# Longformer attention and a SwiGLU block on one core: gathers for two batches, an opening with early scores, and eight attention bursts per batch

## The chip, the core and the metric

The kernel runs on one NeuronCore of a Trainium2 chip. A core has TensorE (PE in the profile: matmuls; PEld is its weight load), VectorE (DVE), ScalarE (ACT), GpSimd (POOL) and SyncE (SP), and 16 DMA engines that move data between HBM and the on-chip memory SBUF. Matmuls write to PSUM, eight banks of 2 KB a partition, which DVE and ACT read. Each engine takes its instructions in program order and waits on semaphores of others. POOL and SP issue the DMAs here. The metric is device time in microseconds (us).

## What is computed

Eight batches of eight heads with 576 tokens and head size 64 go through attention with a sliding window of 32 tokens on either side and eight global tokens, which see and are seen by all. Its output, 4608 rows of 512, goes through a gated FFN of width 1536.

```python
B, H, S, D = q.shape                       # 8, 8, 576, 64
scores = np.matmul(q, k.transpose(0, 1, 3, 2)) / np.sqrt(D)
mask = np.abs(pos[:, None] - pos[None, :]) <= 32
mask = mask | is_global[:, None] | is_global[None, :]
attn = softmax(np.where(mask, scores, -1e9))
x = np.matmul(attn, v).transpose(0, 2, 1, 3).reshape(B * S, H * D)
g = x @ w_gate                             # 512 -> 1536
out = (g * sigmoid(g) * (x @ w_val)) @ w_out
```

## The kernel before

**Units and gaps.** The FFN takes the rows in nine chunks of 512. A chunk is 16 units: twelve gates (`gate`, L702: four matmuls `pg` and four `pv` of 512 columns; then tanh on ACT and two products `gv` and `h` on DVE) and four output strips (`outp`, L769: twelve matmuls `po`, a copy `osb` on ACT and a store on SP). The units are numbered from 0, sixteen a chunk (the first two do nothing, since their work is in the opening). Behind unit n the program puts what `gaps[n]` holds: the steps of the attention of a later batch, which run on TensorE as a burst between two units. The order on every engine is the order of the program (`manual_schedule`, L61).

**One batch of attention** (`attention(b)`, L340) has these steps. `step_T` (batches 1 and 2; batch 0 has `step_T0`) transposes k and q on TensorE, one pair of heads at a time; later batches get them by DMA transposes of a bf16 copy in DRAM. `step_GT` transposes the gathered global rows `kqm`. `step_S2` and `step_SG` are the scores of global queries and global keys, each with an exp on ACT and a mask product on DVE (`p2`, `pg`). `step_P2T` transposes p2, on TensorE or, from batch 4, by a DMA on SP. `step_AV2` multiplies by v and DVE makes `gv` of it. `step_S(0..3)` are the windowed scores of half the heads and half the rows, `step_S(4)` the last 64 rows; each has an exp and a product with `band` on DVE. `step_AV(tp)` makes 128 rows of output from two of these, `gv` and `pg`, and `normalise` on DVE divides into `xa`; `step_AV8` makes the last 64 rows. `step_X` and `step_X8` transpose xa into `xT`, which the FFN reads: on TensorE with an ACT copy in batches 0 and 1, by a DMA on SP later. `vb` (L636) is v shifted by 64 rows, made by two DMAs on SP.

**PSUM.** The pool `pf` has four single banks for the FFN (tag "f"). The pools `psc` (tag "sc") and `pm` (tag "m") hold one tile of two banks each. A step that takes a tile there waits until the last reader of the tile before is through. `mtile` gives batch 0 a tile of pf, later batches one of pm.

**Global rows.** `gather(b)` (L236) issues two indirect DMAs on POOL, one for k and one for q, with the row numbers `gofs[:, b]`. A partition stands for a head and a global token; `gather_mask` (L247) multiplies by `mka` so that each pair of heads keeps its own half, on POOL, for batch 0 on DVE. `gofs` is computed by a row of small DVE instructions (L180 to L215).

**The opening.** Ahead of unit 0, batch 0 runs as a list written by hand (L654 to L665), in which `M(...)` places the mask products and normalisations (`p*`, `xa*`) apart from their steps. `warm(n)` are matmuls on ones whose result nobody reads. Then `first_gates` (L720) begins the FFN with the rows that are ready. POOL issues the loads in this order: k and q of the first four heads, k of the other four, the two gathers, q of the other four, v, two thirds of w_gate and w_val, and then `loads_b` (L284): k and q of batch 1, the last third of the weights, the gather of batch 1, v, and w_out.

Of the kernel before, what the change touches and what calls it, by code (L numbers as in the profile page):

```python
# [9 lines left out]
FP32 = mybir.dt.float32  # L10
BF16 = mybir.dt.bfloat16
I32 = mybir.dt.int32
# [14 lines left out]
def kernel(  # L27
# [112 lines left out]
    def load_0(name, hg):  # L140
# [12 lines left out]
                   allow_small_or_imprecise_dtypes=True)  # L153
    bofs_f = const.tile([P, B], FP32)
    nc.gpsimd.iota(bofs_f, pattern=[[H * S, B]], base=0, channel_multiplier=0,
                   allow_small_or_imprecise_dtypes=True)
# [7 lines left out]
    ones = const.tile([P, CH], BF16)  # L164
    nc.vector.memset(ones, 1.0)
    act0 = const.tile([P, 1], FP32)
# [3 lines left out]
    nc.vector.memset(mt[:, WIN + S : KC], 0.0)  # L170
    def clear(i):
        nc.vector.memset(kT_bufs[i][:, :, 0:WIN], 0.0)
        nc.vector.memset(kT_bufs[i][:, :, WIN + S : KC], 0.0)
        nc.vector.memset(va_bufs[i][:, :, :, D : D + 2], 0.0)
        nc.vector.memset(va_bufs[i][:, :, :, D : D + 1], 1.0)
        nc.vector.memset(va_bufs[i][0:WIN, 0, :, :], 0.0)
        nc.vector.memset(va_bufs[i][P - WIN : P, 4, :, :], 0.0)

# [10 lines left out]
    dmask = const.tile([P, HP, 2], FP32)  # L189
    gofs = const.tile([P, B], I32)  # L190

    nc.vector.tensor_tensor(out=dmask, in0=oh16[:, :, 0, :], in1=oh16[:, :, 1, :], op=ALU.add)
    dmh = const.tile([P, 2, 2], FP32)
    nc.vector.tensor_tensor(out=dmh, in0=dmask[:, 0:2], in1=dmask[:, 2:4], op=ALU.add)
    clear(0)
    tmp8h = const.tile([P, NG], FP32)
# [18 lines left out]
    nc.vector.tensor_scalar(out=gofs, in0=bofs_f, scalar1=hrow, scalar2=None, op0=ALU.add)  # L215
    mka = const.tile([P, 2, 2], FP32)
    nc.vector.tensor_reduce(
        out=mka, in_=oh16.rearrange("p h a r -> p a r h"), axis=AX.X, op=ALU.add
    )
    asel = const.tile([P, 2], FP32)  # L220
    nc.vector.tensor_reduce(out=asel, in_=mka, axis=AX.X, op=ALU.add)
    R2 = (WIN + 0.5) ** 2
# [12 lines left out]

    def gather(b):  # L236
        kg = gw.tile([P, D], FP32, tag="kg", name="kg")
        qg = gw.tile([P, D], FP32, tag="qg", name="qg")
        for dst, src in ((kg, k), (qg, q)):
            nc.gpsimd.indirect_dma_start(  # L240
                out=dst, out_offset=None,
                in_=src.rearrange("b h s d -> (b h s) d"),
                in_offset=bass.IndirectOffsetOnAxis(ap=gofs[:, b : b + 1], axis=0),
            )
        return kg, qg, gw.tile([P, 2, 2, D], BF16, tag="kqm", name="kqm")

    def gather_mask(kg, qg, kqm, eng=None):  # L247
        for a, src in ((0, kg), (1, qg)):
            (eng or nc.gpsimd).tensor_tensor(
                out=kqm[:, a], in0=bc(src, [[0, 2], [1, D]]),  # L250
                in1=bc(mka[:, a, :], [[1, 2], [0, D]]), op=ALU.mult,
            )
        return kqm

# [12 lines left out]

    kqms = [None] * B
    g0 = gather(0)
    load_0("q", 1)  # L270
    load_v(0)
# [11 lines left out]
    load_wgv(1)  # L283
    def loads_b():  # L284
        loaded[1] = new_qk()
        load_qk_part(1, loaded[1], 0)
        load_qk_part(1, loaded[1], 1)
        load_wgv(2)
        g1 = gather(1)
        load_v(1, range(0, 3))  # L290
        kqms[1] = gather_mask(*g1)
        load_v(1, range(3, 5))
        for i in range(4):
            nc.gpsimd.dma_start(
                out=wo_sb[:, 3 * i : 3 * i + 3, :],
                in_=moe_w_out[3 * P * i : 3 * P * (i + 1), :].rearrange(
                    "(fc p) m -> p fc m", p=P
                ),
            )
# [40 lines left out]
    def attention(b):  # L340
# [50 lines left out]
        def step_GT():  # L391
# [200 lines left out]
        def step_X(tp):  # L592
# [19 lines left out]
            nc.scalar.copy(out=xT[:, :, c0 : c0 + P], in_=ps)  # L612

        def step_X8():
            if b >= XB:
# [23 lines left out]
        def vb0(t):  # L639
            st["vb"] = load_vb(0)  # L640
            nc.vector.tensor_copy(out=st["vb"][0:64, 0:2], in_=va[64:128, 0:2])
            nc.vector.tensor_copy(out=st["vb"][64:128, 0:2], in_=va[0:64, 1:3])
            nc.sync.dma_start(out=st["vb"][0:64, 2:4], in_=va[64:128, 2:4])
            nc.sync.dma_start(out=st["vb"][64:128, 2:4], in_=va[0:64, 3:5])

        L = lambda f, *a: (lambda: f(*a))
        if b == 0:
# [3 lines left out]
            def kqm0():  # L651
                kqms[0] = gather_mask(*g0, eng=nc.vector)
# [43 lines left out]

# [112 lines left out]
    def gather_now(b):  # L809
        held[b] = gather(b)  # L810

    def mask_now(b):
        kqms[b] = gather_mask(*held[b])

# [66 lines left out]
```

## Time and profile before

| | |
|---|---|
| median of 4 runs | 366.82 us (366.18 to 368.96) |
| the profiled execution | 365.92 us |
| its span, first to last instruction | 364.2 us |
| granted TensorE clock in the records | 1.000 |
| busy: PE, DVE, ACT, POOL | 350.7, 233.4, 153.4, 97.5 us |

The profile's page cuts the span into 40 slices and gives each engine's busy share in tenths. Of the page, these are the rows of TensorE, DVE and POOL:

```profile
PE   3799999999999999999999999999999999999996
DVE  6666686368934884588548854885488638724850
POOL 7934545924544001540245024100000000000000
```

A slice is 9.1 us. TensorE is busy in all but the first two and the last. The costliest groups of instructions (line, engine, operation, tiles, shapes, count; then busy us and mean ns of one; then the engine's idle time before it) begin so:

```profile
L713 PE MATMUL pg<-xT,wg_sb 128*128 128x512 bf16 x420 | 108.3, 380 | 0.0
L713 PE MATMUL pv<-xT,wv_sb 128*128 128x512 bf16 x420 | 107.8, 379 | 0.0
L746 DVE SCALAR_TENSOR_TENSOR gv<-th,pg 128x512 bf16<-128x512 bf16 x107 | 73.3, 685 | 40.5 <-ACT th L744 39.7
L744 ACT ACTIVATE th<-pg 128x512 bf16<-128x512 f32 x107 | 63.9, 598 | 79.5 <-PE pg L713 69.8
L774 PE MATMUL po<-wo_sb,h 128*128 128x512 bf16 x420 | 94.5, 379 | 0.0
```

Matmuls overlap, so the 380 ns of one is not the time between two of them. How many instructions a group has and the starts in the timeline tell that time.

### The profile page before, as it was taken

The page shows a single profiled execution, that of the slowest core. Times are in us where ns is not written, and L with a number is a line of the kernel's source. Part 1 is how long each engine was busy: PE and PEld are TensorE (multiplying, and loading weights), DVE is VectorE, ACT ScalarE, POOL GpSimd, SP SyncE. Part 2 cuts the span into 40 slices and gives each one's busy share as a digit, 9 for nine tenths or more (in the row PEclk, how much of TensorE's full clock was granted, in tenths as well). Part 3 has the DMA queues.
Part 4 walks back from the last instruction along what each step waited for, and adds up shares of the span by engine and source line. Part 5 has one row for each costly group of instructions (what it writes and reads, how often), then busy time and mean ns, then how long its engine had stood idle before and what let it go on. Part 6 is the DMA issues. An engine that isn't in the chain of part 4 may idle for free.

```text
span 364.2 us, 7867 instructions
## 1 busy us (share of the span) xinstructions
PE 350.7 (96%) x3226; PEld 171.2 (47%) x3226; DVE 233.4 (64%) x469; ACT 153.4 (42%) x238; POOL 97.5 (27%) x114
## 2 busy tenths in 40 slices
PE   3799999999999999999999999999999999999996
PEld 2556444554444454444444444444444444444444
DVE  6666686368934884588548854885488638724850
ACT  5635673457323551345225532452254333323322
POOL 7934545924544001540245024100000000000000
DMA  7999999999999927999999998932350131011002
GB/s 105 141 209 204 132 194 199 185 204 146 138 171 173 187 55 115 138 148 153 153 136 139 142 149 145 165 71 58 116 88 0 45 117 23 0 59 58 0 13 104
DMA packets 141636, 43.51 MB, mean 119 GB/s; under 512 B 126368, under 2 KB 135840, under 8 KB 141600
## 3 DMA queue, kind: packets, MB, share of 16 engines
q0 software_dynamic: 93824, 19.40, 63.2%
q1 hardware_dynamic: 47776, 23.60, 31.6%
q8 instruction: 25, 0.41, 0.5%
q14 instruction: 11, 0.09, 0.1%
HBM read 38.28 MB, written 15.34 MB: 147 GB/s over the span
## 4 chain that ended last, share of the span: by engine, by line
PE 84%; DMA 10%; POOL 3%; DVE 1%; issue 1%; ACT 0%; DVEq 0%; POOLq 0%
PE po L774 25%; PE pg L713 24%; PE pv L713 23%; DMA kg<-in_k_dram,gofs 4%; DMA wg_sb<-in_moe_w_gate_dram 3%; PE ps_av L557 3%; PE ps_s L495 3%; DMA vb<-va 2%; POOL va L102 1%; PE ps_av L548 1%; DMA va<-in_v_dram 1%; PE po L761 1%; PE ps_t L377 1%; PE ps_av L464 1%; PE ps_s L429 1%
## 5 line engine op out<-in xcount | busy, mean ns | idle before, releaser
L713 PE MATMUL pg<-xT,wg_sb 128*128 128x512 bf16 x420 | 108.3, 380 | 0.0
L713 PE MATMUL pv<-xT,wv_sb 128*128 128x512 bf16 x420 | 107.8, 379 | 0.0
L746 DVE SCALAR_TENSOR_TENSOR gv<-th,pg 128x512 bf16<-128x512 bf16 x107 | 73.3, 685 | 40.5 <-ACT th L744 39.7
L744 ACT ACTIVATE th<-pg 128x512 bf16<-128x512 f32 x107 | 63.9, 598 | 79.5 <-PE pg L713 69.8
L774 PE MATMUL po<-wo_sb,h 128*128 128x512 bf16 x420 | 94.5, 379 | 0.0
L750 DVE TENSOR_TENSOR h<-gv,pv 128x512 bf16<-128x512 bf16 x107 | 73.6, 688 | 11.5 <-PE pg L713 0.5
L713 PEld LDWEIGHTS <-wv_sb 128*128 128x128 bf16 x424 | 41.5, 98 | 50.0
L774 PEld LDWEIGHTS <-h 128*128 128x128 bf16 x420 | 39.9, 98 | 46.4
L102 POOL DMA_DIRECT2D va<-in_v_dram x40 | 35.3, 990 | 95.5 <-PE ps_av L557 86.6
L713 PEld LDWEIGHTS <-wg_sb 128*128 128x128 bf16 x424 | 37.0, 98 | 40.9 <-issue 1.7
L779 ACT ACTIVATE osb<-po 128x512 f32<-128x512 f32 x35 | 20.9, 597 | 81.2 <-PE po L774 79.2
L503 ACT ACTIVATE pe<-ps_s 128x1024 bf16<-128x1024 f32 (+1 forms) x40 | 37.5, 939 | 18.2 <-PE ps_s L495 17.4
L509 DVE TENSOR_TENSOR pt<-pe,band 128x1024 bf16<-128x1024 bf16 (+1 forms) x40 | 25.5, 637 | 21.1 <-ACT pe L503 20.6
L524 DVE TENSOR_REDUCE den<-ps_av 128x8 f32<-128x16 f32 (+1 forms) x40 | 6.7, 169 | 35.7 <-PE ps_av L557 33.0
L530 DVE TENSOR_TENSOR xa<-ps_av,den 128x512 bf16<-128x512 f32 (+1 forms) x40 | 25.5, 638 | 1.6 <-DMA xT<-xa 0.2
L495 PEld LDWEIGHTS <-kT 64*128 64x128 bf16 x576 | 11.3, 98 | 15.9 <-issue 14.8
L495 PE MATMUL ps_s<-qT,kT 64*128 64x64 bf16 x576 | 16.2, 196 | 1.1 <-ACT pe L503 1.1
L557 PE MATMUL ps_av<-va,pt 128*64 128x66 bf16 x256 | 15.0, 202 | 0.0
L557 PE MATMUL ps_av<-vb,pt 128*64 128x66 bf16 x256 | 14.8, 202 | 0.1
L109 POOL DMA_DIRECT2D qf<-in_q_dram x5 | 14.0, 2802 | 0.0
L557 PEld LDWEIGHTS <-pt 128*64 128x64 bf16 x512 | 11.4, 114 | 4.6 <-issue 0.7
L109 POOL DMA_DIRECT2D kf<-in_k_dram x5 | 11.4, 2285 | 6.4 <-DMA qf<-in_q_dram 6.2
(123 smaller groups left out, 214.4 us busy)
## 6 DMA issues: line engine op xcount, KB each, us to landing
out_dram<-osb SPq DMA_DIRECT2D x35, 256.0 KB, 2.1
vb<-va SPq DMA_DIRECT2D x14, 264.0 KB, 4.6
va<-in_v_dram POOLq DMA_DIRECT2D x24, 128.0 KB
kf<-in_k_dram POOLq DMA_DIRECT2D x5, 576.0 KB, 10.0
qf<-in_q_dram POOLq DMA_DIRECT2D x5, 576.0 KB, 19.5
k_bf<-in_k_dram POOLq DMA_DIRECT2D x6, 288.0 KB
q_bf<-in_q_dram POOLq DMA_DIRECT2D x6, 288.0 KB, 4.3
va<-in_v_dram POOLq DMA_DIRECT2D x16, 96.0 KB, 10.6
```

Source lines behind the costliest of these rows:

```text
L102: nc.gpsimd.dma_start(out=va[lo:hi, u, :, 0:D], in_=vs[t0 + lo : t0 + hi])
L109: nc.gpsimd.dma_start(out=t, in_=src[b].rearrange("h s d -> s h d"))
L495: nc.tensor.matmul(out=ps[:, par, 64 * slot : 64 * slot + 64], lhsT=kT[r : r + 64, hp, 64 * t : 64 * t + P], rhs=qTs[b][r : r + 64, hp, 64 ...
L503: nc.scalar.activation(out=pe, in_=ps[:, :, 0 : 64 * ns].rearrange("p r (s c) -> p r s c", c=64), func=AF.Exp, scale=SCALE,)
L509: mult = lambda: nc.vector.tensor_tensor(out=pt.rearrange("p r s c -> p (r s) c"), in0=pe.rearrange("p r s c -> p (r s) c"), in1=bc(band, ...
L530: nc.vector.tensor_tensor(out=xa.rearrange("p (g h) d -> p g h d", g=g), in0=bc(ps, pst + [[1, D]]), in1=bc(den, [[4, g], [1, 4], [0, D]]) ...
L557: nc.tensor.matmul(out=ps[64 * e : 64 * e + 64, hg, hl, :], lhsT=pt[:, hl % 2, 4 * (hl // 2) + 2 * (tp % 2) + e, :], rhs=(va if e == 0 els ...
L713: nc.tensor.matmul(out=ps[:, 0:n], lhsT=w[:, cc, P * fc : P * (fc + 1)], rhs=xT[:, cc, t0 : t0 + n], start=(cc == 0), stop=(cc == NCC - 1),)
L744: nc.scalar.activation(out=th[:, 0:n], in_=pg[:, 0:n], func=AF.Tanh, scale=0.5)
L746: nc.vector.scalar_tensor_tensor(out=gv[:, 0:n], in0=th[:, 0:n], scalar=1.0, in1=pg[:, 0:n], op0=ALU.add, op1=ALU.mult,)
L750: nc.vector.tensor_tensor(out=st["h"][:, fc, 0:n], in0=gv[:, 0:n], in1=pv[:, 0:n], op=ALU.mult)
L774: nc.tensor.matmul(out=po, lhsT=st["h"][:, fc, P * ts : P * (ts + 1)], rhs=wo_sb[:, fc, :], start=(fc == 0), stop=(fc == NFC - 1),)
```

## The change

The gathers: `gather(i)` serves batches 2i and 2i+1. `bofs_f` and `gofs` get a row for k and one for q; the partitions that hold the unused half of a head pair are given the row numbers of the next batch (`hb`), so the k gather brings k rows of one batch in one half and of the next in the other, and `gather_mask(b, ...)` picks by `(a + b) % 2`. `step_GT` swaps the halves of odd batches in two copies. `mka` and `asel` are computed ahead of `gofs`. `kqm` has four buffers. The opening's first gather follows the second q load, and batch 1 has no gather of its own; its mask runs on POOL at the start of `loads_b`.

The opening: two blocks of scores, S(0) and S(2), run right behind the first four heads' transposes, the other heads' k copies go to DVE, both their q copies to ACT. `clear` is split: batch 1's memsets go to POOL (in `loads_b`), batch 0's k borders and `ones` move into `tables_a`. The second half of `vb` is made by two ACT copies, not by two DMAs on SP. Five warm matmuls stand where there were four.

The bursts: in batches 1 and 2, and from 3 on, the steps are grouped into fewer gaps. Batch 1 begins one gap later (3, not 2) and transposes xa two strips at a time (`step_X01`). From batch 3 the gap numbers are written out. Tiles: S2 of batch 0 and S4 of batch 2 take psc; AV of batches 1 and 2 takes psc for tp = 2 alone; `step_X01` takes psc. `xa` has four buffers. The loads of k and q of batch 2 move from gap 5 to 7.

```diff
-    bofs_f = const.tile([P, B], FP32)
-    nc.gpsimd.iota(bofs_f, pattern=[[H * S, B]], base=0, channel_multiplier=0,
+    bofs_f = const.tile([P, 2, B // 2], FP32)
+    nc.gpsimd.iota(bofs_f, pattern=[[0, 2], [2 * H * S, B // 2]], base=0, channel_multiplier=0,
...
-    gofs = const.tile([P, B], I32)
+    gofs = const.tile([P, 2, B // 2], I32)
...
-    clear(0)
+    mka = const.tile([P, 2, 2], FP32)
+    asel = const.tile([P, 2], FP32)
+    va_clear(0)
+    hb = const.tile([P, 2], FP32)
+    nc.vector.tensor_scalar(
+        out=hb, in0=bc(asel[:, 1:2], [[-1, 2]]), scalar1=float(H * S), scalar2=None, op0=ALU.mult
+    )
+    nc.vector.tensor_tensor(
+        out=bofs_f, in0=bofs_f, in1=bc(hb, [[1, 2], [0, B // 2]]), op=ALU.add
...
-    def gather(b):
+    def gather(i):
-        for dst, src in ((kg, k), (qg, q)):
+        for a, (dst, src) in enumerate(((kg, k), (qg, q))):
-                in_offset=bass.IndirectOffsetOnAxis(ap=gofs[:, b : b + 1], axis=0),
+                in_offset=bass.IndirectOffsetOnAxis(ap=gofs[:, a, i : i + 1], axis=0),
+    def gather_mask(b, kg, qg, eng=None):
+        kqms[b] = gw.tile([P, 2, 2, D], BF16, tag="kqm", name="kqm", bufs=4)
+                out=kqms[b][:, a], in0=bc(src, [[0, 2], [1, D]]),
+                in1=bc(mka[:, (a + b) % 2, :], [[1, 2], [0, D]]), op=ALU.mult,
+            )
...
+    load_0("q", 1)
     g0 = gather(0)
-    load_0("q", 1)
...
     def loads_b():
+        kT_clear(1, nc.gpsimd)
+        va_clear(1, nc.gpsimd)
+        gather_mask(1, *g0)
         loaded[1] = new_qk()
         load_qk_part(1, loaded[1], 0)
         load_qk_part(1, loaded[1], 1)
         load_wgv(2)
-        g1 = gather(1)
-        load_v(1, range(0, 3))
-        kqms[1] = gather_mask(*g1)
-        load_v(1, range(3, 5))
+        load_v(1)
...
+        nc.vector.memset(ones, 1.0)
+        kT_clear(0)
...
-            nc.vector.tensor_copy(out=st["gT"], in_=ps)
+            if b % 2 == 0:
+                nc.vector.tensor_copy(out=st["gT"], in_=ps)
+                return
+            cols = "p t (h a x) -> p (t h) a x"
+            dst, src = (t.rearrange(cols, h=HP, a=2) for t in (st["gT"], ps))
+            for a in range(2):
+                nc.vector.tensor_copy(out=dst[:, :, a], in_=src[:, :, 1 - a])
...
-            pool, tag = (pm, "m") if b == 0 else (psc, "sc")
-            ps = pool.tile([P, 2, 512], FP32, tag=tag, name="ps_s2")
+            ps = psc.tile([P, 2, 512], FP32, tag="sc", name="ps_s2")
...
-            pool, tag = (pm, "m") if b == 0 and u in (2, 3) or b == 2 and u == 4 else (psc, "sc")
+            pool, tag = (pm, "m") if b == 0 and u in (2, 3) else (psc, "sc")
...
-            st["xa", tp] = work.tile([P, H, D], BF16, tag="xa", name="xa", bufs=3)
+            st["xa", tp] = work.tile([P, H, D], BF16, tag="xa", name="xa", bufs=4)
             if b == 0:
                 pool, tag = (pm, "m") if tp % 2 else (psc, "sc")
             elif b < XQ:
-                pool, tag = (psc, "sc") if tp and (b < XB or tp % 2) else (pm, "m")
+                pool, tag = (psc, "sc") if tp == 2 else (pm, "m")
...
+        def step_X01(n):
+
+            ps = psc.tile([P, 2, 2, HP, P], BF16, tag="sc", name="ps_x")
+            for i in range(2):
...
+            c0 = S * b + 2 * P * n
+            nc.scalar.copy(
+                out=xT[:, :, c0 : c0 + 2 * P].rearrange("p h (i c) -> p i h c", i=2),
+                in_=ps[:, :, 0],
+            )
...
-            nc.sync.dma_start(out=st["vb"][0:64, 2:4], in_=va[64:128, 2:4])
-            nc.sync.dma_start(out=st["vb"][64:128, 2:4], in_=va[0:64, 3:5])
+            nc.scalar.copy(out=st["vb"][0:64, 2:4], in_=va[64:128, 2:4])
+            nc.scalar.copy(out=st["vb"][64:128, 2:4], in_=va[0:64, 3:5])
...
-                L(step_T0, "k", 0, act), L(step_T0, "k", 1, act), L(tables_b), L(clear, 1),
+                L(step_T0, "k", 0, act), L(step_T0, "k", 1, act), L(tables_b),
                 L(step_T0, "q", 0, act), L(step_T0, "q", 1, dve),
-                L(step_T0, "k", 2, act), L(step_T0, "k", 3, act), kqm0, L(step_GT),
-                L(step_S, 0), L(step_S2), M("p2*"), L(step_T0, "q", 2, dve),
-                L(step_T0, "q", 3, act), L(step_P2T), L(step_SG), L(step_S, 1), M("p*", 0),
-                L(vb0, 0), M("pg*"), L(step_AV2), M("p*", 1),
-                L(step_S, 2), L(step_S, 3), L(warm, 2), L(step_AV, 0), M("p*", 2), M("xa*", 0),
-                L(step_AV, 1), L(warm, 1), M("p*", 3), M("xa*", 1), L(step_X, 0),
-                L(step_AV, 2), L(warm, 1), M("xa*", 2), L(step_X, 1), L(step_AV, 3), M("xa*", 3),
+                L(step_S, 0), L(step_S, 2),
+                L(step_T0, "k", 2, dve), L(step_T0, "k", 3, dve), kqm0,
+                L(step_T0, "q", 2, act), L(step_T0, "q", 3, act), L(step_GT),
+                L(step_S2), L(step_SG), M("p*", 0), M("p2*"), M("pg*"),
+                L(step_S, 1), L(step_P2T), L(step_S, 3), L(vb0, 0), L(warm, 1),
+                M("p*", 1), L(step_AV2), L(warm, 2), M("p*", 2),
+                L(step_AV, 0), M("xa*", 0), L(step_AV, 1), L(warm, 1), M("p*", 3), L(step_X, 0),
+                L(step_AV, 2), L(warm, 1), M("xa*", 1), M("xa*", 2), L(step_X, 1),
+                L(step_AV, 3), M("xa*", 3),
...
-            [L(step_S, 2)],
-            [L(step_S, 3), L(step_AV, 0)],
-            [L(step_AV, 1), L(step_X, 0)],
-            [L(step_AV, 2), L(step_X, 1)],
-            [L(step_AV, 3), L(step_X, 2)],
-            [L(step_X, 3), L(step_S, 4)],
+            [L(step_S, 2), L(step_AV, 0)],
+            [L(step_S, 3), L(step_AV, 1)],
+            [L(step_AV, 2)],
+            [L(step_AV, 3), L(step_X01, 0)],
+            [L(step_X01, 1), L(step_S, 4)],
+        ] if b < XB else [
+            [L(step_S2), L(step_SG)],
+            [L(step_P2T), L(step_S, 0)],
+            [L(step_S, 1), L(step_AV2)],
+            [L(step_S, 2), L(step_AV, 0), L(step_X, 0)],
+            [L(step_S, 3), L(step_AV, 1), L(step_X, 1)],
+            [L(step_AV, 2), L(step_X, 2)],
+            [L(step_S, 4), L(step_AV, 3), L(step_X, 3)],
         ]
...
-        return [
-            [L(step_GT), vb],
-            [L(step_S2), L(step_SG)],
-            [L(step_S, 0), L(step_P2T)],
-            [],
-            [L(step_S, 1), L(step_AV2)],
-            [L(step_S, 2)],
-            [L(step_S, 3), L(step_AV, 0), L(step_X, 0)],
-            [L(step_AV, 1), L(step_X, 1)],
-            [L(step_S, 4), L(step_AV, 2), L(step_X, 2)],
-            [L(step_AV, 3), L(step_AV8), L(step_X, 3), L(step_X8)],
-        ]
+        return {
+            1: [L(step_GT), vb],
+            2: [L(step_S2), L(step_SG)] + ([L(step_P2T)] if b >= XP else []),
+            4: [L(step_S, 0)] + ([] if b >= XP else [L(step_P2T)]),
+            7: [L(step_S, 1), L(step_AV2)],
+            9: [L(step_S, 2), L(step_AV, 0), L(step_X, 0)],
+            11: [L(step_S, 3), L(step_AV, 1), L(step_X, 1)],
+            12: [L(step_S, 4), L(step_AV, 2), L(step_X, 2)],
+            14: [L(step_AV, 3), L(step_AV8), L(step_X, 3), L(step_X8)],
+        }
...
-    at(5, qk_now, 2)
-    for b, o in ((1, 2), (2, 15)):
+    at(7, qk_now, 2)
+    for b, o in ((1, 3), (2, 15)):
         for i, g in enumerate(attention(b)):
...
-        for i, g in enumerate(steps):
-            slot = o + 1 + (16 * i) // len(steps)
-            gaps[slot] = gaps.get(slot, []) + g
+        for i, g in steps.items():
+            gaps[o + i] = gaps.get(o + i, []) + g
...
-        g_at[b] = o - 16 + 6
-        m_at[b] = o - 16 + 13
+        if b % 2 == 0:
+            g_at[b] = o - 16 + 6
+            m_at[b] = o - 16 + 13
```

More of the change, by code (lines that the diff above doesn't have):

```diff
@@ L164 @@
     ones = const.tile([P, CH], BF16)
-    nc.vector.memset(ones, 1.0)
     act0 = const.tile([P, 1], FP32)
@@ L170, with kT_clear, va_clear @@
     nc.vector.memset(mt[:, WIN + S : KC], 0.0)
[L171 to L177, printed above, removed]
+    def kT_clear(i, eng=nc.vector):
+        eng.memset(kT_bufs[i][:, :, 0:WIN], 0.0)
+        eng.memset(kT_bufs[i][:, :, WIN + S : KC], 0.0)
+    def va_clear(i, eng=nc.vector):
+        eng.memset(va_bufs[i][:, :, :, D : D + 2], 0.0)
+        eng.memset(va_bufs[i][:, :, :, D : D + 1], 1.0)
+        eng.memset(va_bufs[i][0:WIN, 0, :, :], 0.0)
+        eng.memset(va_bufs[i][P - WIN : P, 4, :, :], 0.0)
     oh16 = const.tile([P, HP, 2, 2], FP32)
@@ L194 @@
     nc.vector.tensor_tensor(out=dmh, in0=dmask[:, 0:2], in1=dmask[:, 2:4], op=ALU.add)
-    clear(0)
+    mka = const.tile([P, 2, 2], FP32)
+    nc.vector.tensor_reduce(
+        out=mka, in_=oh16.rearrange("p h a r -> p a r h"), axis=AX.X, op=ALU.add
+    )
+    asel = const.tile([P, 2], FP32)
+    nc.vector.tensor_reduce(out=asel, in_=mka, axis=AX.X, op=ALU.add)
+    va_clear(0)
[6 more added lines that the diff above has]
+    )
     tmp8h = const.tile([P, NG], FP32)
@@ L215 @@
     nc.vector.tensor_scalar(out=gofs, in0=bofs_f, scalar1=hrow, scalar2=None, op0=ALU.add)
[L216 to L221, printed above, removed]
     R2 = (WIN + 0.5) ** 2
@@ L242, in gather @@
                 in_=src.rearrange("b h s d -> (b h s) d"),
-                in_offset=bass.IndirectOffsetOnAxis(ap=gofs[:, b : b + 1], axis=0),
+                in_offset=bass.IndirectOffsetOnAxis(ap=gofs[:, a, i : i + 1], axis=0),
             )
-        return kg, qg, gw.tile([P, 2, 2, D], BF16, tag="kqm", name="kqm")
-    def gather_mask(kg, qg, kqm, eng=None):
+        return kg, qg
+    def gather_mask(b, kg, qg, eng=None):
+        kqms[b] = gw.tile([P, 2, 2, D], BF16, tag="kqm", name="kqm", bufs=4)
         for a, src in ((0, kg), (1, qg)):
             (eng or nc.gpsimd).tensor_tensor(
-                out=kqm[:, a], in0=bc(src, [[0, 2], [1, D]]),
-                in1=bc(mka[:, a, :], [[1, 2], [0, D]]), op=ALU.mult,
+                out=kqms[b][:, a], in0=bc(src, [[0, 2], [1, D]]),
+                in1=bc(mka[:, (a + b) % 2, :], [[1, 2], [0, D]]), op=ALU.mult,
             )
-        return kqm
     wg_sb = wpool.tile([P, NCC, DF], BF16)
@@ L612, in step_X @@
             nc.scalar.copy(out=xT[:, :, c0 : c0 + P], in_=ps)
+        def step_X01(n):
+            ps = psc.tile([P, 2, 2, HP, P], BF16, tag="sc", name="ps_x")
+            for i in range(2):
+                for hp in range(HP):
+                    nc.tensor.transpose(
+                        out=ps[:, i, 0, hp, :],
+                        in_=st["xa", 2 * n + i][:, 2 * hp : 2 * hp + 2, :].rearrange(
+                            "p h d -> p (h d)"
+                        ),
+                        identity=ident,
+                    )
+            c0 = S * b + 2 * P * n
+            nc.scalar.copy(
+                out=xT[:, :, c0 : c0 + 2 * P].rearrange("p h (i c) -> p i h c", i=2),
+                in_=ps[:, :, 0],
+            )
         def step_X8():
@@ L651, in kqm0 @@
             def kqm0():
[L652 removed]
+                gather_mask(0, *g0, eng=nc.vector)
             return [
                 L(squares), L(tables_a),
[L656 removed]
+                L(step_T0, "k", 0, act), L(step_T0, "k", 1, act), L(tables_b),
                 L(step_T0, "q", 0, act), L(step_T0, "q", 1, dve),
[L658 to L664 removed]
+                L(step_S, 0), L(step_S, 2),
[7 more added lines that the diff above has]
+                L(step_AV, 3), M("xa*", 3),
             ], [L(step_X, 2)], [L(step_X, 3)], [L(step_S, 4), M("p*", 4)], [L(step_AV8)], [L(step_X8)]
@@ L809, in gather_now @@
     def gather_now(b):
-        held[b] = gather(b)
+        held[b] = gather(b // 2)
     def mask_now(b):
-        kqms[b] = gather_mask(*held[b])
+        for i in range(2):
+            gather_mask(b + i, *held[b])
     def qk_now(b):
```

## The prediction

> **What bounds the kernel.** I read first who waited for whom on TensorE over the whole span (us in total, times, longest):
>
> ```profile
> PE ps_t L357 <- DMA k_bf<-in_k_dram: 6.1, 1, 6.1
> PE ps_s L495 <- ACT pe L503: 1.1, 1, 1.1
> PE ps_g L395 <- DVE kqm L249: 0.9, 1, 0.9
> PE ps_g L395 <- POOL kqm L249: 0.7, 1, 0.7
> PE ps_p2t L454 <- DVE p L441: 0.5, 1, 0.5
> PE ps_t L357 <- ACT qT L363: 0.5, 1, 0.5
> PE ps_t L377 <- ACT qT L386: 0.3, 1, 0.3
> PE pg L731 <- ACT xT L612: 0.2, 1, 0.2
> ```
>
> All but the POOL row and the 0.3 lie before 30 us; beyond, TensorE is the bound, and its time is the FFN plus the attention bursts between its units. So three things count: when the FFN starts, what a burst costs, and whether a burst is made to wait. Next the timeline in batch 2, and the rows at the end of the head (start, length, engine, line):
>
> ```profile
> 87.72 1.03 PE L713 MATMUL pv<-xT,wv_sb 128*128 128x512 bf16 x4
> ...
> 88.68 0.41 PE L495 MATMUL ps_s<-qT,kT 64*128 64x64 bf16 x16
> 88.82 0.18 DVE L479 TENSOR_TENSOR gvt<-lo,gvt 128x4 bf16<-128x4 f32 x1
> ...
> 89.02 1.04 PE L713 MATMUL pg<-xT,wg_sb 128*128 128x512 bf16 x4
> ...
> 89.89 1.03 PE L713 MATMUL pv<-xT,wv_sb 128*128 128x512 bf16 x4
> ...
> 90.85 0.41 PE L495 MATMUL ps_s<-qT,kT 64*128 64x64 bf16 x16
> 91.10 0.28 PE L548 MATMUL ps_av<-gvt,pg 64*128 64x264 bf16 x2
> ...
> 91.69 1.04 PE L713 MATMUL pg<-xT,wg_sb 128*128 128x512 bf16 x4
> 92.56 1.03 PE L713 MATMUL pv<-xT,wv_sb 128*128 128x512 bf16 x4
> ...
> 94.11 0.39 PE L713 MATMUL pg<-xT,wg_sb 128*128 128x512 bf16 x1
> ```
>
> ```profile
> 24.36 0.75 POOL L263 DMA_DIRECT2D wv_sb<-in_moe_w_val_dram  x1 [2.35 <-DMA wv_sb<-in_moe_w_val_dram]
> 24.72 0.62 PE L606 MATMUL ps_x<-ident,xa 128*128 128x128 bf16 x4
> 25.38 0.59 ACT L612 COPY xT<-ps_x 128x512 bf16<-128x512 bf16 x1 [1.39 <-PE ps_x L606]
> 26.02 0.60 PE L731 MATMUL pg<-xT,wg_sb 128*128 128x256 bf16 x4
> ```
>
> From the second I take burst prices. The chain of waits has "PE po L774 x48" in 10.36 us: 0.216 us a matmul, so four pv take 0.86 and a gate of eight 1.73. The pv from 87.72 should hand over at 88.58; the next pg starts at 89.02, so a burst of scores alone costs 0.44. Scores with AV: 91.69 - 90.75 = 0.94. AV alone: 94.11 - 93.42 = 0.69. Apart 1.13, together 0.94: **a merged burst saves 0.2 us**. From the third: the FFN starts (26.02) when the second xT copy is done (25.97).
>
> **The steps.**
>
> *Bursts.* Batches 3 to 7 go from nine to eight bursts (the empty list step was never one): 5 x 0.2 = 1.0. Batch 1 loses the lone scores burst, one merge from the pair transposes and T0 sharing a gap with batch 0's AV8; batch 2 gains about as much less: by adding the bursts' prices gap by gap, 27 bursts become 24, 0.6 gained. **Sum -1.6.**
>
> *Gathers.* Sixteen gathers of about 1.0 us on POOL become eight; POOL waits 86.6 us for va buffers, so only batch 1 feels it. There the burst with GT waits for kqm: pg to pg 38.56 to 42.28 is 3.72, its twin in batch 2 (73.98 to 76.89) 2.91. The mask now comes from the first gather, long landed: **-0.8**. With the gather goes what stood behind it on POOL: v(1)'s last two issues waited until 41.37. They follow directly now, vb(1) lands earlier, and the S3+AV0 burst's DMA wait (1.43 against 1.14 between its FFN neighbours and those of its twin) goes: **-0.3**. kqm needs four buffers and has them; odd batches' GT copies twice (0.29 becomes about 2 x 0.2 on DVE), a whole gate ahead of its reader: nothing.
>
> *Opening.* DVE makes gofs later: mka and asel (0.17, 0.16) move ahead of it and hb and bofs join (two of the 0.15 kind), while ones and kT_clear leave; about 0.55 later. POOL idled 0.76 us before the gather and now issues q1's 0.76 there, so the gather starts near 6.0 instead of 5.5 and its rows still land before the mask is wanted. I walked the new order with the old durations on PE, ACT and DVE in turn. q hp1's copy on DVE loses clear(1) ahead of it and ends at 9.96 (11.24 before), so S0 starts at 10.0 instead of 11.9; S(2) follows at once and the old wait of 1.1 for its exp goes. But T0 k2, k3 come behind them, with copies on DVE (to 13.3), so kqm is made at 13.2 instead of 11.2 and p2 at 16.2 instead of 14.2. From there exp1 (1.02) and p2t (0.69) follow on ACT to 18.5, AV2 ends 19.3, gv 20.1, AV0 starts near 20.2. The same walk over the old order puts AV0 at 20.8, measured 20.49; so **0.6 to 0.7 earlier**, and the same at the second xT copy. The rest is covered: ACT's two vb copies (1056 columns, about 1.05 each by the exp over 1024) end by 21.7, wanted at 23; the two SP copies of vb leave the DMA engines; weights allow up to 2.1, as wv's first third has landed by 24.36 and pv first ran at 26.45. **-0.7**, bounds -1.3 and +0.3.
>
> [...] In the head 512-column matmuls of "warm" take 0.43 to 0.52, later 0.216; the row of AV changes from 0.92 a strip to 0.59 only at 25.3, after TensorE had hardly paused since 19.0, some 6 us. [...] I take the row.
>
> *Memsets on POOL.* clear(1), six memsets, now runs there near 17 us, beside DVE's chain. [...] The row: POOL's kqm (0.40, at 40.67 and 41.03) ran beside a DVE product at 41.06 that took 0.69, its usual mean. [...]
>
> *Waits that are added.* Both 2-bank PSUM pools hold one tile. **(a)** Batch 1's gap 14 now has the pair transposes and S4 both in psc. S4 must wait until ACT has copied 1024 columns out (about 1.0 by exp's 1.02; 0.59 for 512), behind osb's 0.6, and the whole FFN queues behind it on TensorE. Nearest row: ps_s <- ACT pe, 1.1. I take 1.2, bounds 0.9 and 1.4. **(b)** AV0 and AV1 of batches 1 and 2 now sit in neighbouring gaps, both in pm (AV1 was in psc). Put AV0 at the 88.68 burst: gv ends at 89.00, so AV0 waits 0.1 to 0.2. DVE then has tt to 90.38, p2 to 90.97, AV0's normalise (0.17+0.20+0.69 and gaps, 1.1) to 92.0; AV1 would start at 91.7: 0.35. **(c)** In batch 2 S4 moved from pm to psc, one gate behind AV2' there: DVE goes on with a gate (1.4) to 93.4, p3 94.0, AV1's normalise 95.1, a gate 96.5, AV2's normalise 97.6, S4 wanted at 96.9: 0.65; AV8 behind AV3 in pm 0.3. DVE is busy in this stretch already:
>
> ```profile
> 86.00:101.00 15.00, 15.00 (x197) 7.19 (x196) 13.85 (x31) 6.74 (x10) 5.80 (x7) 1.00 2.00 139
> ```
>
> (fifth number: DVE 13.85 of 15 us.) Merging bursts takes 0.4 us out of a stretch that DVE nearly fills. Sum: (a) 1.2, batch 1 0.5, batch 2 0.15+0.35+0.65+0.3 = 1.45: **+3.1**, bounds 1.7 and 5.5. In batches 3 to 7 a gate lies between AV0 and AV1, and AV2 follows AV1 by an output strip of 2.59 us: none.
>
> *Covered moves.* qk loads of batch 2 go from gap 5 to 7, past the gather at 6, on POOL: four issues of 0.7, wanted at 70 us. P2T's transpose for batch 4 on is queued on SP at gap 2 instead of 4; outputs behind it wait for p2, about 1.5 us, and have six osb buffers; AV2 comes at gap 7. X0 to X3 transposes move up by at most one gap.
>
> **Sum:** -1.6 -0.8 -0.3 -0.7 +3.1 = -0.3 us on the profiled execution's 365.92 (span 364.2 and 1.7 around it). The median shown is 366.82, 0.9 above it, so the forecast is **366.5**. What can be told from no change here is about 0.5%, 1.8 us.
>
> **Rivals.**
>
> [...]
>
> *DVE lags by one more gate (slower).* If in the stretches of batches 1 and 2 DVE is one gate's two products (0.68+0.69) further behind than walked, each chain of AV0, AV1, S4 ends 1.4 later: +2.8, net +2.5, so 369.3. It decides the sign from 0.15 a batch and passes what can be measured from 1.05. For: DVE 13.85 of 15. Against: DVE's starts in my walk of the old order agree with the trace within 0.1.
>
> *The gather still binds.* If one gather can't serve batch 1 in time, 0.8 stays: 367.3, inside "no change"; it was issued near 6 us and is wanted near 40, so 0.03.
>
> **Numbers.** No measurable change 0.40 (with the late gather), small waits 0.32, lagging DVE 0.28. Range 363.8 to 369.3: the low end is the head at its best with 1.7 of waits (-1.6-1.1-1.3+1.7 = -2.3, and 0.7 of spread between runs), the high end the lagging DVE. The likeliest case's own range is 365.2 to 368.2.
>
> **What would show it.** In the waits: ps_s <- ACT xT near 1.2 in batch 1, ps_av <- DVE xa near 0.35 twice, ps_s <- DVE xa in batch 2, and ps_g <- POOL kqm gone. The first pg of the FFN near 25.3. From 112 us a chunk should take 37.1, not 37.3. Wrong would be: waits on TensorE under 2 or over 5 us past 30 us, or an FFN start outside 24.7 to 26.3.

## The result, and the profile after

The changed kernel takes **366.02 us** (median of 42 runs, 364.25 to 367.6); the kernel before took 368.1 in the runs beside it (median of 63). The ratio is 0.9939, with a 95% interval of 0.9926 to 0.9952: 0.6% faster, just beyond the 0.5% that can be told from no change. The forecast was 366.5, no change likeliest. The two profiled executions differ by less: 365.92 and 364.8 us, spans 364.2 and 363.1, so -1.1. The forecast was counted from 366.82, a median of four runs; the 63 runs put the kernel before 1.3 higher. So the small distance of 366.02 from 366.5 is in part luck: the forecast difference was -0.3, the measured one -2.1.

On the page of the kernel after, the busy times and the rows of slices:

```profile
PE 348.3 (96%) x3227; PEld 170.8 (47%) x3227; DVE 233.2 (64%) x470; ACT 154.9 (43%) x237; POOL 90.5 (25%) x112
...
PE   3899999899999999999999999999999999999996
...
DVE  6677685268924894588548863887388727814750
...
POOL 8964549530290001600174011000000000000000
```

TensorE's row is fuller in slice 2 (8 for 7) and dips to 8 in slice 8: the opening is tighter, and a new wait stands there, at about 66 us. POOL is 7 us less busy.

Who waited for whom on TensorE, after (us in total, times, longest):

```profile
PE ps_t L367 <- DMA k_bf<-in_k_dram: 6.3, 1, 6.3
PE ps_s L510 <- ACT xT L642: 1.1, 1, 1.1
PE ps_s L510 <- ACT qT L373: 0.7, 1, 0.7
PE ps_x L621 <- DVE xa L545: 0.7, 2, 0.3
PE ps_s L510 <- DVE xa L545: 0.5, 1, 0.5
PE ps_s L444 <- DVE gT L411: 0.4, 1, 0.4
PE ps_av L563 <- DVE xa L545: 0.4, 2, 0.2
PE ps_s L510 <- ACT p2e L451: 0.3, 1, 0.3
PE ps_g L405 <- DVE kqm L258: 0.3, 1, 0.3
PE ps_av L479 <- DMA p2t<-p: 0.3, 1, 0.3
PE pg L771 <- ACT xT L627: 0.2, 1, 0.2
PE ps_av L591 <- DVE xa L545: 0.2, 1, 0.2
```

The POOL row for kqm and the opening's wait for an exp are gone. In their place stand the wait of S4 for the paired xT copy (1.1) and waits for DVE's xa: 0.7 in the opening, and in batches 1 and 2 two of 0.2 for AV1, 0.5 for S4 and 0.2 for AV8. The largest looks so in the timeline (start, length, engine, line; in brackets the idle time and who ended it):

```profile
64.60 0.61 PE L634 MATMUL ps_x<-ident,xa 128*128 128x128 bf16 x8
64.80 0.60 ACT L819 ACTIVATE osb<-po 128x512 f32<-128x512 f32 x1 [1.58 <-PE po L814]
...
65.29 1.01 ACT L642 COPY xT<-ps_x 128x1024 bf16<-128x1024 bf16 x1
66.35 0.29 PE L510 MATMUL ps_s<-qT,kT 64*128 64x64 bf16 x8 [1.14 <-ACT xT L642]
...
19.91 0.29 PE L563 MATMUL ps_av<-gvt,pg 64*128 64x264 bf16 x2
20.50 0.29 PE L563 MATMUL ps_av<-gvt,pg 64*128 64x264 bf16 x2
...
24.52 0.60 PE L771 MATMUL pg<-xT,wg_sb 128*128 128x256 bf16 x4
```

S4 (the line at 66.35) could not start until ACT had done an `osb` and then 1024 columns. The last three lines are from the end of the opening. The same strips before (timeline):

```profile
20.49 0.40 PE L548 MATMUL ps_av<-gvt,pg 64*128 64x264 bf16 x2
21.41 0.40 PE L548 MATMUL ps_av<-gvt,pg 64*128 64x264 bf16 x2
...
25.27 0.29 PE L548 MATMUL ps_av<-gvt,pg 64*128 64x264 bf16 x2
```

AV0 starts at 19.91 (20.49 before), AV1 0.59 behind it (0.92 before), and the FFN at **24.52** against 26.02. TensorE works at its later speed from the first AV strip on; in the kernel before it did so only at the fourth, at 25.27.

The starts of the same gate in both traces, after minus before, say where the time went: first gate -1.5; second chunk -1.1; third -0.6; fourth -0.8; last chunk -1.2. The opening is gained, batches 1 and 2 give most of it back, and the later chunks gain what their merged bursts save.

### The profile page after: what moved, and what is told of

It is laid out like the page before. It is cut to its first block, busy times and chain, and to the rows that moved or that the text cites. A ratio compares the mean times of both kernels' runs of the same rounds, so it can differ in the third digit from the quotient of the medians.

```text
span 363.1 us, 7859 instructions
## 1 busy us (share of the span) xinstructions
PE 348.3 (96%) x3227; PEld 170.8 (47%) x3227; DVE 233.2 (64%) x470; ACT 154.9 (43%) x237; POOL 90.5 (25%) x112
## 4 chain that ended last, share of the span: by engine, by line
PE 83%; DVE 9%; DMA 4%; ACT 3%; issue 1%; POOL 0%; DVEq 0%; POOLq 0%
PE po L814 25%; PE pg L753 22%; PE pv L753 21%; PE ps_s L510 3%; PE ps_av L572 2%; DMA p2t<-p 2%; DVE h L790 2%; DVE gv L786 2%; DVE pt L524 2%; DVE xa L545 1%; DMA k_bf<-in_k_dram 1%; PE ps_t L387 1%; PE ps_av L563 1%; PE ps_s L444 1%; PE ps_av L479 1%
## 5 line engine op out<-in xcount | busy, mean ns | idle before, releaser
L753 PEld LDWEIGHTS <-wg_sb 128*128 128x128 bf16 x424 | 38.0, 98 | 42.9 <-issue 1.7
L572 PE MATMUL ps_av<-va,pt 128*64 128x66 bf16 x256 | 14.2, 197 | 0.0
```

The lines of the kernel that those rows point to most:

```text
L572: nc.tensor.matmul(out=ps[64 * e : 64 * e + 64, hg, hl, :], lhsT=pt[:, hl % 2, 4 * (hl // 2) + 2 * (tp % 2) + e, :], rhs=(va if e == 0 els ...
L753: nc.tensor.matmul(out=ps[:, 0:n], lhsT=w[:, cc, P * fc : P * (fc + 1)], rhs=xT[:, cc, t0 : t0 + n], start=(cc == 0), stop=(cc == NCC - 1),)
```

## The experiments

**How much do executions of one kernel differ?** The kernel before, unchanged.

> The kernel before, unchanged, for another look at one execution. The runs of before spread from 365.6 to 370, and its profiled execution was one of the fast ones (365.92). Theory A (the clock of TensorE in the opening opens at a moment that varies from execution to execution): the first FFN matmul starts at another time than 26.0 us or the first FFN matmuls run slowly, and from 60 us on the two traces have the same steps. Theory B (DMA landings vary): the waits in batch 1 for kqm or vb (0.8 and 0.3 us) differ by 1 us or more.

It took 367.58 us, span 365.9: 1.7 more than in the profile shown. Its waits on TensorE:

```profile
PE ps_t L357 <- DMA k_bf<-in_k_dram: 6.9, 2, 6.5
...
PE ps_av L557 <- DMA vb<-va: 1.1, 1, 1.1
PE ps_av L464 <- DMA p2t<-p: 0.7, 1, 0.7
...
PE ps_av L464 <- DMA va<-in_v_dram: 0.5, 1, 0.5
```

k came later, the FFN started at 26.93, and vb, p2t and va, which cost nothing or 0.3 in the profile shown, were waited for. The strips turned fast at the fourth (its first two matmuls take 0.29 from 26.19, those of the three before 0.40), as in the profile shown, so this second execution speaks for the landings (theory B) and not for the clock (theory A). The profile of before on which the sum rests is one with lucky landings (365.92, where all its runs but one lie between 365.62 and 371.72).

**The parts alone**, each put into the kernel before. The opening's order, split `clear`, `vb` by ACT, gather behind q:

> Before with the opening of the changed kernel alone (order of the list, q load ahead of the gather, memsets, vb by ACT, tile of S2), gathers and gaps as before. Theory A (clock opens at about 20 us, since TensorE hardly pauses from 14.4 us): FFN starts near 24.5 us, AV strips at 0.59 us each, 1.3 to 1.6 us off the profiled span and 0.4% or more off the time. Theory B (order alone, slow clock to 25 us): FFN start near 25.3, 0.7 us. Theory C (the gain comes from gathers and gaps): within 0.2 us of before.

365.91 us, ratio 0.9957 (0.9932 to 0.9981), span 363.9; the FFN starts at 24.74, 1.3 before that of before, as theory A had it. But its first two AV strips, from 19.80, are still slow (0.40 and 0.92 apart), and only the third is fast (0.29 at 22.41). The waits for the mask (0.6) and for batch 1's vb (0.4) stay, as they belong to the gather.

The gaps and tiles of the bursts:

> Before with the new gaps and PSUM tiles for batches 1 to 7 alone; opening and gathers as before. Theory A (bursts give 1.6 us, added waits for PSUM tiles take 3.1): GT one gap later no longer waits for kqm (-0.8), so +0.5 us, between 0 and +1.0; S4 of batch 1 waits 1.1 to 1.2 us for ACT. Theory B (waits are small, bursts decide): 1.5 to 2.5 us faster.

367.76 us, ratio 1.0007 (0.9982 to 1.0033). The new waits come just as in the full change (ps_s for ACT xT 1.1, for DVE xa 0.5). Against before, its gates start 0.3 later at the first, 1.1 at the second chunk, 1.7 at the third, and 0.6 at the end: 1.1 comes back in the later chunks. Its second chunk would have been later still, but the wait for kqm is gone here too: batch 1 begins a gap later. So two parts of the change remove the same 0.8, and it counts once.

The gathers:

> Before with one gather for two batches alone; opening and gaps as before. Theory A (kqm wait 0.8 and vb wait 0.3 of batch 1 go, everything else is covered): 0.8 to 1.1 us faster, FFN start 26.0 or up to 0.6 later for the later gofs (then 0.3 to 0.5 faster). Theory B (the gathers matter for all batches through POOL and DMA): over 1.5 us faster, with a difference from 112 us on.

366.74 us, ratio 0.9996 (0.9967 to 1.0024). From the first gate (+0.2) to the second chunk (-1.2) it gains 1.4, against 1.1 in the sum; then it loses it:

```profile
PE ps_av L476 <- DMA p2t<-p: 1.6, 2, 1.1
```

The DMA transposes of p2 in batches 4 and 5 landed 9.5 and 8.8 us after their issue here, and TensorE is ready for AV2 8.4 us after it. In the other profiles that time them, batches 4 and 5 take 7.1 to 9.3 us and batches 6 and 7 only 2.4 to 3.8. A gain ahead of such a race is not safe.

**Late bursts alone**: the written gaps for batches 3 to 7 (and the fourth xa buffer), nothing else.

```diff
-        return [
-            [L(step_GT), vb],
...
+        return {
+            1: [L(step_GT), vb],
...
+        for i, g in steps.items():
+            gaps[o + i] = gaps.get(o + i, []) + g
```

> Before with the gaps of batches 3 to 7 alone (eight bursts, not nine). Theory A (a merged burst saves 0.2 us and nothing waits for it): each chunk from 112 us on 0.2 us shorter, 1.0 us off from chunk 2 to the end, 0.25% of the time, less what the p2t transposes of batches 4 and 5 happen to wait. Theory B (P2T issued earlier also removes waits of AV2 for p2t): 1.5 us or more; SP issues p2t directly behind p2 in either order, so I doubt it.

365.9 us, ratio 0.9968 (0.9949 to 0.9986). Its gates stand 0.82 behind those of before at the third chunk and 0.20 ahead at the end: 1.02 for five batches, where 5 x 0.2 was forecast. The 1.3 that its FFN started late comes from another thing, to which the clock's experiments return.

**Taking the added waits away.** In the changed kernel the second pair of transposes takes the other pool:

```diff
-            ps = psc.tile([P, 2, 2, HP, P], BF16, tag="sc", name="ps_x")
+            pool, tag = ((psc, "sc"), (pm, "m"))[n]
+            ps = pool.tile([P, 2, 2, HP, P], BF16, tag=tag, name="ps_x")
```

> The changed kernel with the second pair transposes of batch 1 in pm instead of psc, so S4 behind it does not share a tile. Theory A (the wait of S4 for ACT's copy is 1.1 us on the critical path): the wait ps_s <- ACT xT goes, chunk 1 starts 1.0 to 1.2 us earlier (near 69.1 us), and the whole is 0.8 to 1.2 us faster than the changed kernel, 0.9910 or so of before. Theory B (the time comes back at the next wait, DVE being behind): under 0.4 us.

363.73 us, ratio to before 0.9898 (0.9868 to 0.9928), span 363.2. S4 now follows at once, but in the profiled execution something else came in (timeline):

```profile
66.20 0.61 PE L635 MATMUL ps_x<-ident,xa 128*128 128x128 bf16 x8
...
66.74 0.29 PE L510 MATMUL ps_s<-qT,kT 64*128 64x64 bf16 x8
66.89 1.01 ACT L643 COPY xT<-ps_x 128x1024 bf16<-128x1024 bf16 x1
...
43.78 0.64 ACT L392 COPY kT<-ps_t 128x576 bf16<-128x576 bf16 x1 [3.08 <-PE pv L754]
...
45.02 0.46 PE L444 MATMUL ps_s<-kT,gT 128*32 128x320 bf16 x8 [1.51 <-ACT qT L396]
```

ACT stood still for 3.1 us from 40.7, 1.5 of it on the path. The copy needs the transposes `ps_t`, which had ended by 41.7, and not the `pv` named as releaser; what held it stays open. This stall, at 1.5, outweighs the 1.2 that the burst with S4 got shorter, so this execution's span did not move. The profiled execution was the second slowest of the six.

Next, all the added waits at once: also AV1 of batch 1 in the gap of AV2, batch 2 spread with a gate between its AV strips, its AV all in pm:

```diff
-                pool, tag = (psc, "sc") if tp == 2 else (pm, "m")
+                pool, tag = (psc, "sc") if tp == 2 and b < XB else (pm, "m")
...
-            [L(step_S, 3), L(step_AV, 1)],
-            [L(step_AV, 2)],
+            [L(step_S, 3)],
+            [L(step_AV, 1), L(step_AV, 2)],
...
-            [L(step_AV, 2), L(step_X, 2)],
-            [L(step_S, 4), L(step_AV, 3), L(step_X, 3)],
+            [],
+            [],
+            [L(step_S, 4), L(step_AV, 2), L(step_X, 2)],
```

> The changed kernel with pair transposes as in x01_pm, AV1 of batch 1 moved into the gap of AV2, and batch 2 spread over gaps up to 30 in the manner of batches 3 to 7 (seven bursts behind its transposes, AV all in pm, AV8 in psc). Theory A (DVE-bound waits of AV1, S4 and AV8 cost about 0.5 us in batch 1 and 1.3 in batch 2): no wait over 0.2 us on TensorE for xa or gv, 2.5 to 3.2 us faster than the changed kernel, 0.986 of before. Theory B (DVE has as much to do anyway and TensorE waits elsewhere): under 1.3 us faster than the changed kernel.

**362.89 us**, ratio 0.9864 (0.9833 to 0.9894), whose interval lies below that of the change (0.9926 to 0.9952). Its six runs form two groups, 361.8 to 362.0 and 363.8 to 364.2; the profiled one is of the upper and shows the ACT stall again (1.2) and p2t waits of 1.1. With p2 of batches 4 and 5 transposed on TensorE instead (`XP = 4` to `XP = 6`):

> best with p2 of batches 4 and 5 transposed by TensorE and ACT, as in batch 3, and not by a DMA on SP. Theory A (AV2 of these batches waits 0.3 to 1.6 us in all for p2t's landing): the wait for p2t goes, each of the two bursts costs 0.29 us more, so 0.0 to 0.8 us faster than best. Theory B (the waits are rare): 0.5 us slower than best.

362.73 us, ratio 0.987 (0.9838 to 0.9902), span 361.2: the same median, but its four runs lie between 362.71 and 362.92. Beyond 30 us the trace lists no wait of this kernel's TensorE. At the third chunk it is 2.6 us ahead of the changed kernel, though its FFN started 0.3 later: the waits of batches 1 and 2 were worth 2.9 (the 0.14 that AV0 of batch 1 loses stays).

**The clock.** In the opening TensorE's speed shows in the durations alone: the first two matmuls of an AV strip take 0.29 us where it is fast and 0.40 where it is slow, and the records' granted clock reads 1.00 in both (18 to 26 us of before and of after). That the clock is behind it there is my reading. The changed kernel without its warm matmuls, which feed no result:

```diff
-                L(step_S, 1), L(step_P2T), L(step_S, 3), L(vb0, 0), L(warm, 1),
-                M("p*", 1), L(step_AV2), L(warm, 2), M("p*", 2),
+                L(step_S, 1), L(step_P2T), L(step_S, 3), L(vb0, 0),
+                M("p*", 1), L(step_AV2), M("p*", 2),
...
```

> The changed kernel without the five warm matmuls (they compute nothing that is used). Theory A (unbroken work of TensorE opens its clock before the AV strips, and that is part of the 1.5 us that the opening gives): 64-column AV matmuls stay at 0.26 us until 22 us or later, FFN start 0.2 to 0.6 us later than 24.5. Theory B (the order alone): the clock opens as before or it makes no difference, and FFN start is at 24.5 or earlier, up to 0.4, as TensorE has less to do.

367.12 us, ratio 0.9977 (0.9953 to 1.0001), an interval that lies above that of the change. AV0 starts at 19.84, as with them, so the order is as early; but (timeline)

```profile
19.84 0.40 PE L563 MATMUL ps_av<-gvt,pg 64*128 64x264 bf16 x2 [0.88 <-DVE gvt L494]
20.76 0.40 PE L563 MATMUL ps_av<-gvt,pg 64*128 64x264 bf16 x2
...
25.16 1.03 PE L771 MATMUL pg<-xT,wg_sb 128*128 128x256 bf16 x4
25.99 1.06 PE L771 MATMUL pv<-xT,wv_sb 128*128 128x256 bf16 x4
```

an AV strip takes 0.92, none is fast, and even the FFN's first matmuls take 1.03 for four where 0.60 is usual. TensorE turns fast at about 28 (four pv take 1.06 from 25.99 and 0.74 from 28.12), and the third gate is 2.2 us behind that of the changed kernel. TensorE pauses for 0.5, 0.9 and 0.3 us between 17.7 and 22; with the warm matmuls it pauses there for the 0.3 alone.

The reverse: the kernel before with more of them, ahead of step_GT, step_P2T and S3, and nothing else moved.

```diff
-                L(step_S, 2), L(step_S, 3), L(warm, 2), L(step_AV, 0), M("p*", 2), M("xa*", 0),
+                L(step_S, 2), L(warm, 2), L(step_S, 3), L(warm, 2), L(step_AV, 0), M("p*", 2), M("xa*", 0),
```

> Before with four more warm matmuls where TensorE idles between 11 and 19 us. Theory A (the clock): AV matmuls at 0.22 us from about 20.5 us and the FFN starts 0.5 to 0.9 us earlier than in the kernel before (25.1 to 25.5 where AV0 starts at 20.5). Theory B (the order alone matters): FFN start no earlier than 5.4 us after AV0's start, or later for the work added.

368.11 us, ratio 0.9999 (0.9979 to 1.0019). The strips are fast from AV0 on (0.29), and AV0 itself comes at 19.73, 0.76 before that of before, with the old order (next strip 0.69 behind). Then:

```profile
25.59 0.22 PE L557 MATMUL ps_av<-vb,pt 128*64 128x66 bf16 x1 [3.19 <-DMA vb<-va]
...
26.62 0.40 PE L548 MATMUL ps_av<-gvt,pg 64*128 64x264 bf16 x2
27.54 1.03 PE L731 MATMUL pg<-xT,wg_sb 128*128 128x256 bf16 x4
```

The third strip waits 3.2 us for the second half of vb, and 1.0 us behind the wait's end TensorE is slow again: the matmuls of the strip at 25.59 still take 0.22, the one at 26.62 has 0.40. By windows of 4 us (third number from the end of a row: granted clock):

```profile
22.00:26.00 4.00, 0.81 (x20) 0.53 (x20) 1.16 (x4) 0.59 (x1) 1.25 (x2) 1.00 1.21 230
26.00:30.00 4.00, 4.00 (x40) 2.87 (x39) 2.14 (x6) 0.70 (x2) 1.03 (x1) 0.57 1.28 204
```

The kernel with the late bursts alone shows the same 0.57 in 26 to 30, behind a vb wait of 1.79 (slow again from 26.4, 0.9 us after the wait): that is its late start. So I gave the warmed kernel the vb copies of the change, too (two ACT copies behind S3):

> Before with the four more warm matmuls of before_warm and vb's second half by ACT (behind S(3)). Theory A (clock and vb are the two things that the opening needs, the order of scores matters little): AV matmuls at 0.22 us from 20 us, no wait for vb, FFN start 24.6 to 25.2, 0.8 to 1.4 us faster than before. Theory B (the order of the scores is what counts): FFN start 25.5 or later.

366.27 us, ratio 0.9969 (0.9948 to 0.9991). The FFN starts at **24.08**, before that of the changed kernel, with the old order of scores. By the third gate it is 1.9 ahead of before; then it waits 0.7 for q of batch 1 and 1.3 at step_GT for the mask, since batch 1 still has its own gather, whose rows landed at 40.3: 0.4 is left. So the opening's time came here from TensorE's speed (0.29 from AV0 on) and from `vb` (a wait of 0.21 for 3.19), without the new order of scores.

Last, the changed kernel with vb by DMA again:

> The changed kernel with the second half of batch 0's vb by two DMAs on SP as before, and not by ACT. Theory A (the two DMAs land at 23 to 26 us behind the loads and would stop the AV strips, as before_warm shows): AV of the third strip waits 1 to 3 us for vb, FFN start at 25.5 or later, TensorE's clock closes again in some executions, 1 to 3 us slower than the changed kernel. Theory B (they land in time, since the loads run earlier): under 0.4 us.

365.5 us, ratio 0.9957 (0.9933 to 0.9981), which doesn't tell it from the change itself. Neither theory fits its profile: the third strip waits 0.24 for vb, AV0 comes 0.4 later, and the FFN starts at 25.20, 0.7 later. But the mean granted clock of single executions does tell them apart: **of its 12, five are at 0.995, with a median of 366.73 us against 365.08 for the other seven**. Of the changed kernel's 44 listed executions none is under 0.998; of 80 of the kernel before, 17 are at 0.995 or lower, with a median of 368.65 against 367.32. In the two profiled executions at 0.995, those of late_groups and before_warm, the loss is the granted clock of 0.57 behind the wait for vb (0.57 for 4 us of 364 makes 0.995). The profile of after_vbdma is of an execution at 1.00, so for its five that place is argued and not shown. And the lower mean is not seen with a DMA-made `vb` alone: the opening alone has four of 12 at 0.995 and the warmed kernel with vb by ACT three of 12, though ACT makes their batch 0 `vb`. Both still wait for batch 1's own gather and `vb` (0.6 and 0.4, and 1.3 and 0.2 in their profiles); where in those executions the clock fell stays open.

## Why the prediction came out as it did

The time lay within its range and near its middle, with the luck of the baseline above. That no change could be told was the likeliest case and did not come: the change was faster by a little more than that, mainly through one term that was too small.

**The bursts (-1.6): the late ones confirmed, the early ones half.** The late ones gave 1.02 alone for the 1.0 of the sum. In batches 1 and 2, where 0.6 was forecast, the 27 bursts of before, less their waits, come to 20.6 us on TensorE and the 24 of after to 20.2: 0.3.

**The gathers (-0.8 and -0.3): right in kind, 1.4 for 1.1**, alone up to the second chunk. The 0.8 was too small because the twin in batch 2, with which it was compared, held a wait of its own (0.3, for ACT's copy of qT, in the list of waits that the prediction shows). The burst with GT took 1.98 in before and 0.84 in after: 1.1. These two misses of 0.3 cancel, which is luck. The wait for the mask is removed by the later start of batch 1 as well, which the sum did not see.

**The added waits (+3.1): confirmed.** (a) was 1.14 idle, 1.2 by the burst's length, for 1.2. Measured by how much longer the bursts are than their unwaited forms, batch 1's strips lost 0.14 and 0.36 (0.5), batch 2's 0.14, 0.36, 0.6 and 0.23 (0.15, 0.35, 0.65, 0.3): 3.0 in all, and 2.9 came back when they were taken away. What these steps paid for a PSUM pool with one tile was what its reader still had queued, and walking DVE instruction by instruction gave it within 0.1. The lagging-DVE rival (+2.8) falls with this. So does the case of small waits (0.32), since 3.0 came.

**The opening (-0.7): the step that failed, in its size.** The order came as walked: AV0 0.58 earlier for 0.6 to 0.7, and 0.65 where the strips stayed slow (after_nowarm). What the 0.7 lacks is TensorE's speed. The prediction took the row of before, whose strips are fast only at 25.27; here they were fast at 19.91, and the gain was **1.5**. The FFN start, 24.52, also lies outside the 24.7 to 26.3 that the prediction named. No run or trace that the prediction had shows the 1.3 in the term's bounds, from which the range's low end is added up; the runs since showed 1.5 here, 1.3 with the opening alone and 0.9 without the warm matmuls. The row of before was one opening, fast 6.3 us after a pause of 1.12 that ended at 18.98. In the changed kernel 19.91 is 3.9 us after TensorE's last pause (0.33, ended 15.97) and 5.5 after the one before it (0.38, ended 14.44), and before_warm is fast at 19.73, 0.9 after a pause of 0.58: no one count from the last pause fits the three. Without the warm matmuls the 1.5 shrinks to 0.9 at the FFN's start, and by the third gate that kernel is 0.7 behind before. With the measured terms the sum reads -0.3 and -1.0 (bursts), -1.4 (gathers), -1.5 (opening), +3.0 (waits), and -0.3 for the qT wait of batch 2, which the other profiles with the old opening don't have: -1.5. The gates of the last chunk differ by 1.2, since p2t's 0.3 goes against it.

**Covered at nothing: one that wasn't.** "The two SP copies of vb leave the DMA engines" was taken as a relief of no price. It takes away a landing that TensorE sometimes waits for just when its strips have turned fast (3.19 us in before_warm, 1.79 in late_groups), and in these two profiles the granted clock was 0.57 from 26 to 30, behind that pause. With the two DMAs put back, five executions of twelve are at the lower clock (0.995) and 1.65 us longer.

**POOL's memsets: nothing, and the sum has no term for them.** They ran from 16.3 to 18.7 beside DVE's chain. One of two vb copies there took 0.73, but such copies take 0.43 to 0.80 with and without memsets beside them (0.70 and 0.71 in gathers_alone, which has none; 0.43 and 0.47 in after_nowarm, which has them). DVE was free again at 18.95, before the matmuls of AV2 ended (about 19.0), so AV0 was not late by it.

**Profile and median.** The medians differ by 2.1, the profiles by 1.1. Five executions with the old opening start their FFN at 26.02, 26.93, 26.33, 26.23 and 27.29 (mean 26.56), five with the new at 24.52, 24.74, 24.48, 24.66 and 24.85 (24.65): 1.9, not 1.5. With that, and without the chance wait for qT, the sum is -1.6, a little less than the interval's 1.8 to 2.7. The rest would be in landings like those of the second execution of before; how often each comes was not measured.

## What to carry to other kernels

Where a change makes a sum of terms that cancel, look for the one that depends on a state (here TensorE's speed in the opening): fill TensorE's pauses ahead of its first long stretch (without the five warm matmuls the FFN started 0.64 later here), and take landings that may be late away from just behind it (with vb's two DMAs put back, five executions of twelve were 1.65 us longer). Before two steps in neighbouring gaps share a single PSUM tile, add up what the tile's reader has queued; giving the second step the other pool made its burst 1.2 us shorter, and taking away all such waits made a kernel of 362.9, 1.4% below the start. And take a median's distance from the profiled execution as a warning: the one shown may lack the waits that the others have.

## What the hardware showed unexpectedly

- TensorE turned fast at different times in the same opening, in one profile of each kernel: with AV0 at 19.86 to 19.92 in four kernels that share the opening, the strips became fast by 19.9 in two, at about 20.2 in one and between 22.1 and 22.7 in one. In a fifth, the opening alone, it was about 22.1. Nothing in the opening's program tells the four apart, so the 1.5 of the profile shown is one draw. What sets the instant stays open.
- The page's granted clock says 1.00 in the opening's slow stretch; only the durations (0.40 for 0.29) show it. In after_nowarm it says 1.00 even from 25.2 to 28, where FFN matmuls are slow (1.03 for four). After a pause of 1.79 (late_groups) or 3.19 us (before_warm) it says 0.57. So in these profiles a mean of 0.995 goes with a clock that fell again, and TensorE turning fast late leaves it at 1.00.
- The transpose of p2 by DMA landed after 9.5, 8.8, 2.5 and 3.6 us for batches 4 to 7 of one execution (gathers_alone). The split between batches 4 and 5 and batches 6 and 7 is the same in every profile that times them; what stands in the way of the first two was not tested.
